# Four interleaved attention layers on one core: GpSimd's long instructions made to wait for VectorE's last short one, the key weights third in the load queue, six extra unread matmuls, and a new written-out order

## The chip, the core and the metric

The kernel runs on one core of a Trainium2 chip. Time is device time of that core in microseconds (us). Five engines work side by side, each through its own list of instructions in the order in which the kernel wrote them: TensorE (PE; its weight loads are listed apart as PEld), VectorE (DVE), ScalarE (ACT), GpSimd (POOL), and SyncE (SP), which here only issues DMAs. They are held together by semaphores. A wait stands at the head of one engine's list, so whatever is queued behind the waiting instruction on that engine waits too.

## The reference

Four layers follow one another on x, 2048 tokens by 512 features: A, B, A, B. Each is normalised first and added to x.

```python
def _A_ref(x, wqkv, wo):            # linear attention, 32 heads of 16
    phi = lambda t: jnp.where(t > 0, t + 1, jnp.exp(t)) + 1e-6
    pq, pk = phi(q), phi(k)
    kv = einsum("bhsd,bhse->bhde", pk, v);  z = einsum("bhsd->bhd", pk)
    o = einsum("bhqd,bhde->bhqe", pq, kv) / (einsum("bhqd,bhd->bhq", pq, z) + 1e-6)
    return o @ wo
def _B_ref(x, wqkv, wo):            # softmax attention in a window of 256 tokens back
    mask = (i - j >= 0) & (i - j < 256)
    p = softmax(where(mask, q @ k.T * 16 ** -0.5, -1e9))
    return (p @ v) @ wo
x = x + A(norm(x)); x = x + B(norm(x)); x = x + A(norm(x)); x = x + B(norm(x))
```

Both A layers use one set of weights, both B layers another.

## The kernel before, in words

The 2048 tokens are cut into 16 tiles of 128, and x stays on the chip throughout. `Plan` writes the whole program down as a graph of some 2500 steps (`Op`), each with an engine or a choice of engines, what it reads and writes, and the PSUM bank tiles that it uses. Four stages can be told apart in time, with their edges running into one another:

- **First A layer.** Per tile `norm` takes statistics (`stats`, `aggr` on VectorE), the inverse root of the variance on GpSimd (`eps`, `pow`), normalises (`xn`, VectorE), and transposes (`T`). `a_k` and `a_q` are matmuls (`k`, `q`), and `phi` makes their feature map by an exponential on ScalarE (`E`) and two VectorE steps (`E1`, `phi`). `g` gathers normalised x times keys.
- **First B layer.** `front` makes the output of the A layer for a tile (`aout`, then `res` adds it to x), its norm, and q, k, v of the B layer (`bq`, `bk`, `bv` on TensorE, then the evictions `bqe`, `bke`, `bve`, each on ScalarE or on VectorE). Keys and values go to a layout of their own by DMAs (`kd`, `vd`, on SP). `b_scores` makes scores (`s`, TensorE) and their exponential (`ex`, ScalarE), and masks the near triangle on VectorE (`mk`). `b_far` does the same for the far 64 columns of the window; its two masks per tile (`mf`) can be on GpSimd (`affine_select`) or on VectorE (a product with a constant triangle). `b_values` multiplies by the values (`pv`), and divides (`rcp`, `div`). `b_out` transposes by DMA (`oT`), multiplies by `wBo` (`bout`) and adds (`res`).
- **Second A layer**, which begins tile by tile behind the first B layer, and **second B layer**, which begins behind that. The last tile ends in `b_last`, and the result leaves by `outp` (GpSimd or SP) and `out` (SP).

What sets the order is not the code but a table. `place` unpacks `TABLE`: two bytes per step give the order of all steps, one byte per step its engine, one byte per tile its PSUM bank. `place` also adds the waits that reuse of a bank needs, and `synchronise` turns all of them into semaphore waits. Each engine then plays its steps in the order of the table. In `setup` the loads are listed as x's first tile, the key weights `wAk`, and so on, but here, too, the order in which SP issues them is the table's. Ten matmuls named `fill` that nobody reads run at the start, from `fill()`, behind nine more that `run` itself writes; a first group of constants is made by GpSimd in `setup`, and the others in `consts` (`c3` to `c24`, and `wp`, which rearranges B's weights).

Of the kernel before, what the change touches and what calls it, by code (L numbers as in the profile page):

```python
# [11 lines left out]
P = 128  # L12
D = 512
# [73 lines left out]

def place(g):
# [116 lines left out]
LATE = 5  # L205
FILL = 10
# [7 lines left out]
class Plan:  # L214
# [33 lines left out]
    def fill(self):  # L248
# [4 lines left out]
        for i in range(FILL):  # L253
            ps = Tile(1, K.cls)
            self.pe("fill", lambda e, ps=ps: e.matmul(K.ps(ps), K.warm[:, 0:P], K.warm, start=True, stop=True), -1000.0, 1, 512, ps=[ps])
            for o in first:
                o.deps.append(self.g.ops[-1])

# [340 lines left out]
    def b_scores(self, j, b, fs, key):  # L599
# [3 lines left out]
        q = P * j + 64 * b  # L603
# [3 lines left out]
        pair = lambda two, free: bass_view(K.PS[:, two[0].banks[0], :], [[512 * (two[1].banks[0] - two[0].banks[0]), 2]] + free)  # L607
# [12 lines left out]
        out = lambda h, m, w: bass_view(K.P(sl)[:, h, fs[0], 384 * b:384 * b + w], [[2816, m], [704, n], [1, w]])  # L620
# [7 lines left out]
        def mk(e):  # L628
            x = out(0, 4, 64)
            return e.tensor_tensor(x, x, K.tri[:, 0, :].unsqueeze(1).unsqueeze(1).to_broadcast([P, 4, n, 64]), ALU.mult)  # L630

        self.on("DVE", "mk", mk, key + 0.02, dve(256 * n, "2x"), rd=[("P", sl, f, b, h) for f in fs for h in range(2)] + [("tri",)], wr=[("P", sl, f, b, 2) for f in fs])

    def b_far(self, j, key):
# [4 lines left out]
        pair = lambda two, free: bass_view(K.PS[:, two[0].banks[0], :], [[512 * (two[1].banks[0] - two[0].banks[0]), 2]] + free)  # L639
# [22 lines left out]
        for b in range(2):  # L662
            def mk(e, eng, b=b):
                x = bass_view(K.P(sl)[:, 0, 0, 384 * b + 256:384 * b + 320], [[704, 16], [1, 64]])
                if eng == "POOL":
                    return e.affine_select(out=x, in_=x, compare_op=ALU.is_ge, fill=0.0, base=-2, pattern=[[0, 16], [-2, 64]], channel_multiplier=1)  # L666
                return e.tensor_tensor(x, x, K.tri[:, 1, :].unsqueeze(1).to_broadcast([P, 16, 64]), ALU.mult)

            engs = {"DVE": dve(1024, "2x")}
            if K.par["gp"]:  # L670
                engs["POOL"] = (1260, 1320)
            else:
                mk = lambda e, mk=mk: mk(e, "DVE")
            self.g.add("mf", engs, mk, key + 0.02 + 0.01 * b, rd=[("F", sl, 0), ("F", sl, 1), ("tri",)], wr=[("F", sl, b, 1)])

    def b_values(self, j, h, key):
# [6 lines left out]
        for f in (2 * h, 2 * h + 1):  # L683
# [66 lines left out]
    def middle(self, ph):  # L750
# [9 lines left out]
        self.rp = 4 if last else 3  # L760
        if last:
# [14 lines left out]
        for j in range(T):  # L776
            if j + 3 < T:
                front(j + 3)
            if j + 1 < T:
                self.b_v(j + 1, (j + 1) % ring, base + j + 1 - par["k_v"])  # L780
            wide = [2, 2]
# [7 lines left out]
            if j + 2 < T:  # L789
                self.b_far(j, base + j + par["k_far"])  # L790
# [26 lines left out]
    r"{cng-pPB;a5@iY{LmoOA>!(E7taWF0tzJi%B3+_NZOpED|QDJ&43`1Zj6oJ?92J&M8EQoI*C%lIS5C+3yIBW=wpaR6h3@E6v5`@S2m;enX#CKpZ0%pWv",
    r"5D^PuB20{#Ff(SstmrT@mW2{f7>i(0EC$7JI26ackPjkZ63h?Ta0Dd9>{t>jVF|2&L7_U<!17oVYhgvq19h-6mV+u-0GeV|tcJ~S1=PlsP!O793v7eKu",
    r"rjp7Rj?ZBVm+*n4e$(9g~r$#&q7IPg5{whHo`T~3U@&e*bRGNFI0r#I08rFIhcu~a5T=s1NZ@E;~cyPV{j~v!?}1L=HYx?h5KMN9>g`c02ktToPcYwEq",
    r";V4cpe@=JKT+X@B&Q5y|@pj;dGpclW;P&$8|UZ*W*JtgpXhYZp2NvA3woTT!tNR5q8AS&;^%cCtQq6@FJFmOL!R%;}HymEAb0l!|Qkj17l|lM1koBuD~",  # L820
    r"F46p!I?Jb^{1C>5ii^awZO7K}_=F$f05VDtnZV-$)?&oDSW$6y$pLQrwIira8Ip2Uz8ieBI?yn{P%C*H){cnVMB87xj`aTlJ$64VvD;d#7^aVQ>@q*8Q",
    r"(PSPp5fTgJ_#icS-jjB@&8b-tEDaNE~@DfK*Xc|ees0JmWFqD+S(kpz8Z}2T9!%>usl4A-yP4Ouu-oyL&08`;Zj7G631*M|TSeD9Bc?w72DJ4aqnpBHw",
    r"(`Xt)V`&^Epfhxq&QU^2M2V>arKaT6jLuUXsz}XgI#r?;G=nZsJ(@`ks4jiMuUMbHVH!$H-!UD%Lm(ugoAd$G(|i1gx9B!SqVY6=m?lyyYC~D6A(g_?*",
    r"qT~WTe?V>=o4P143vo?QZ~v?Ij9jerY58)BQ>R*l$qvG70N<o@CsF?Ni>;qQCTd9^Jp&3r`(i>^3oK_M?#tmSz17juF^GXM^P{;wx?ONh!#?JoK1@<8g",
    r"`)Q*pXJy5{iLKX&J4e<+PG|U>{sV-Ki(8qx@8W)>0@A&AqTU7Nphmh@Q}T3d4n{Foop}w2|)6CVEUy=^eeN&GdnGQhBbx6}b}Mqx<xcD)U`>Ks~4@<-n",
    r"Yn3wu#G4$l#|6Lq1f)SLQHU&@XBs0u%%*c^v%a%akeU1<tO<Vf5XUr~SRhXZIT$K^LPjc@U7-bJrz3vH#{)Qz6e9(qevxf*Yy=k$VJ(si27NjMqrpih*",
    r"PBlBKL!29SkeW9-ug%fd9PR<EAF%P6cG?>!x5E@GRDH^BcX%wAfaCNTD2Pgv{q;#B->+lV#%QHAWZztvyoRU*<YEI8hITJVInLLYUb91i2HMthI<W_u#",
    r"@A5s)%!-9IH(<k-9S7nTe27|eJpM-CDHb>6IoybWk+X1C?#P`v8)xUde3*_<6Yk2yZTLQS;x4?Dm+^9L%kB6m9i#4ioVxKUUd@5IJ$K+99Fre#5YET>x",
    r"d0dB#=MT#@LKN4>$w;A=03cE7jO>F$%S|!&*gbsm=|$>9K=PqC>P^goQJpZ4t~Y2c_Yu~H#`7`;6omW^>`3&=b#*ngYzyPjPX=_wVQKuao)oTR0%H0A-",
    r"FI1<Hh`lA9F~q&ri4%m*#{jk?PNTIk8Hj2Jm1W!iV@U59MLJi8pg&wS_<PRzAYRc?2g_BY7Y<QD3>K+R4pSbM=&4sAv3~NAXJj!r%Bkf8c%GQtjshe2_",  # L830
    r"o#3dL%rQtA`0QliqU6`Vn3RL3}(TCKEN!lT)!@0?tLa>}X{Dy7PzvZ<`<I0sU#)CoSxV|Xl&<5PT^-*R@9L*-O!)JsmKTB~<_hR<?pl}3%{3H*Wss~`$",
    r"h5tUhy%B6y;U@D9{$LG1d>Y#F~x2l-xs0yeHTvQcT?^Gdml;5j7DzEyWKB`Zur^=)Xs=}&`YO6}9b}FALsq(8*s<-;Ada1Rluj;41sCBBeTCc*Y{wkab",
    r"uPUktDx$i`m-sSY;YjK#2Uj6gTGd5$RU1?{wNvd<Bh_v-K!s50)Mz!4`>4n&ii)Z#smiK~8l}ppNnB1%=1yviDyz1rt!kU9s;a4>YPbrmLaBjjkou|yt",
    r"0Ahos-b$Q?y9D$rG}}EYJ}RS4ya9Pv)Zo?s%R>@I;0M(BkCGo=NlYDRZwHqI5l3KQ|HxDrNzhuWhJIUA&I3rd*yygT~HTQZB<8|R%g^%RbCxabyYoeT%",
    r"AxSRbaWK>Z>4fSzS@VWty6<_NuEYsLW8oWTu*>Ldb0OO@){53S^E7DG?--WR{3BQB6{l)gF~aZmYS<Ndq-c1(JrUk-DSqs(b3bdY~Sv$kI%jOKcTILdh",
    r"c)Rko{Z>bi=fZm6khzIq@cJJbRdO%|#}Dz0iF4<)w5kw~&w#g&6{NS3I>GDU@!FcMZCNp8t2kL8Idi7w$JkHnDd@>m^_m=a5}$x%5b`6P#&lG9RHa>`P",
    r"*Or4RUl0b^cS;-~wq_`|sC8dPiROjTp+*0|afE1G_s=aiOr}9j)N<k?k9i_Fjl~U44+DJlqE{P<ul$J8mQj$n3DJ$iqiu9It(pO$cA9*QHReX7-Ua8mW",
    r"xq6|x%Nx~Mx=0x=%P&<|=^_23r_7XDGF!SyIZi6cB)J@y6Vgk{O9iPYmE@$Pkd)G221r#ID1)T3RFmpbLu$%YnJ&}hy?l^bQd{cCQdus8Wtn%xTH*aOS",
    r"tyI-mAsZY@<!522ALs4WT-5bxl&h_$VyoyZ)KQdlzEa$hRbS6Eo)?ijFeF_Ulzzm`6L%)t<;nH@>$k-+u~>$BTBEA4YE<*$wj#&m*t9Fm1|O4Z<5WjMH",
    r")*J5uHZTN>jNmH)O1gldZB%w#y_*Ck>>bOqLz8Pj*Tp*)QW|g4EHwWQy#TiLyub%1yZ?x8;u9m3wkP?n_4fMRMs3`m21C96Fm0tF!CeI*-n)zYFM`I-k",  # L840
    r"y@!|BXAi_WUGHrncfI=?QU>*{*Cy{@kt=vum=ZlpWtj(VUDtUKu-I;akz2kFMTi4Lhd>tNdHrh0~+shjEGx{L0r1L;<}n;xvg>j-*?9;%1w;kvbMquc6",
    r"sx{xlcyXzi$vYw)6>4<uSo~ozmBD%S5p<C)cy07l1i|S%JlrFAI=$^Wl4y{Y-k-E3urKjsKdbS>=FX)SUx89>i>vejA9-!ywxq7|6q{rxSdc2;X$LbI!",
    r"q}itr=y`g+zO1k4l{%COZNixTdV#*Guj%W0m0qn2m}k16DP;ERgF2GFp(E=TdZS*bpX*I}i{7jk>B1(uj-kVvn0m1;Vjk)!I-Ch_9_eHHgkGy3>*G4AU",
    r"ZR)kW%{PRr6=mWI+~89W9!>`jozv!={x$BzN=sBm?oCFr{Cz<rj#zNBbZP6v;LwF>BIVnKB^;{NamaVuAl0cx~M5;w&~*Lt=_J8=!ANwPNcyk*6;Lt9n",
# [179 lines left out]
```

## Time and profile before

| | |
|---|---|
| runs | 420.35, 420.37 and 419.5 us; median 420.35 |
| profiled execution | span 418.7 us from the first to the last instruction; its own time outside the profiler isn't given, and the median lies 1.65 us above the span, the lowest run 0.8 us |
| TensorE busy | 395.0 us, 94% |
| VectorE busy | 352.5 us, 84% |
| ScalarE busy | 345.2 us, 82% |
| GpSimd busy | 137.6 us, 33% |
| granted TensorE clock | 0.995 on the mean |

Busy time is the time in which the engine has an instruction in work. Matmuls overlap one another in the record (a 512-column one is shown with 380 ns, and the next starts 216 ns after it), so a busy TensorE isn't one at its peak. The chain of waits is followed back from the last instruction: each piece is what released the next one. A row of the timeline gives start, duration, engine, line and operation, and in brackets the idle time of the engine before it and what ended that. Lines are those of the kernel before. L382 is all matmuls with tokens as rows (`k`, `v`, `aout`, `bv`, `bout`), L396 those with features as rows (`q`, `bq`, `bk`), L614 and L649 near and far scores, L691 `pv`; L624 and L658 the exponentials; L630 `mk`, L667 `mf` on VectorE, L666 `mf` on GpSimd, L347 `xn`, L406 `E1`.

### The profile page before, as it was taken

What the parts mean: (1) busy time and instruction counts of PE and PEld (TensorE: products, weight loads), DVE (VectorE), ACT (ScalarE), POOL (GpSimd) and SP (SyncE); (2) the same over time, 40 slices, a digit from 0 to 9 for tenths busy, and PEclk for the clock granted to TensorE, in tenths of its full rate; (3) what the DMA queues carried; (4) which work ended last, traced back from release to release, by engine and by line L of the source; (5) the groups of instructions that cost most, each with busy time, mean ns of one, the idle gap of its engine ahead of it and who ended that gap; (6) DMA issues with size and microseconds to landing.
All of it is one profiled execution on the core that took longest, in us unless ns stands there. A gap on an engine that the chain in (4) does not pass through costs nothing.

```text
span 418.7 us, 17187 instructions
## 1 busy us (share of the span) xinstructions
PE 395.0 (94%) x7549; PEld 258.8 (62%) x7549; DVE 352.5 (84%) x788; ACT 345.2 (82%) x428; POOL 137.6 (33%) x227
## 2 busy tenths in 40 slices
PE   8999999999999999999999999999999988989975
PEld 3644775776575567465567677676667646657634
DVE  6997899989989898988886989898898696866655
ACT  3524459999999999889996247999999999999983
POOL 5578522140433252311603302321234241243011
PEclk9999999999999999999999999999999999999989
DMA  7675025432344345343232002343324333244552
GB/s 233 196 176 139 2 71 126 104 92 55 78 92 92 80 99 100 77 100 87 67 68 39 16 2 78 73 98 93 80 54 117 81 80 80 53 122 127 129 95 64
DMA packets 67842, 37.81 MB, mean 90 GB/s; under 512 B 48248, under 2 KB 62968, under 8 KB 67768
## 3 DMA queue, kind: packets, MB, share of 16 engines
q1 hardware_dynamic: 67472, 35.93, 35.5%
q8 instruction: 59, 0.97, 1.0%
q0 software_dynamic: 288, 0.79, 0.6%
q14 instruction: 15, 0.12, 0.1%
q10 hardware_dynamic: 8, 0.00, 0.0%
HBM read 6.29 MB, written 2.10 MB: 20 GB/s over the span
## 4 chain that ended last, share of the span: by engine, by line
PE 54%; ACT 28%; DVE 10%; DMA 4%; issue 2%; POOL 1%; SPq 1%; POOLq 0%; ACTq 0%
PE ps L382 19%; ACT pb L624 18%; PE ps L396 14%; PE ps L691 9%; PE ps L614 5%; ACT pb L658 4%; ACT vp L624 4%; PE ps L457 3%; DVE stats L343 2%; DMA xres<-in_A_x_dram 1%; ACT vp L658 1%; DMA oT<-o 1%; DVE pb L630 1%; DVE tE L406 1%; DVE xres L550 1%
## 5 line engine op out<-in xcount | busy, mean ns | idle before, releaser
L624 ACT ACTIVATE pb<-ps 128x1024 bf16<-128x1024 f32 (+2 forms) x224 | 207.6, 1024 | 9.9 <-PE ps L614 8.7
L691 PEld LDWEIGHTS ps<-vB,pb 128*128 128x128 bf16 x2560 | 77.7, 96 | 12.3 <-issue 4.6
L691 PE MATMUL ps<-vB,pb 128*128 128x34 bf16 x2560 | 82.9, 178 | 1.7 <-DVE vS L371 0.7
L345 POOL TENSOR_SCALAR ve<-mv 128x1 f32<-128x1 f32 x64 | 15.4, 240 | 189.8 <-DVE mv L344 188.3
L396 PE MATMUL ps<-xT,wBp 128*128 128x128 bf16 x1024 | 69.3, 220 | 1.6 <-ACT pb L624 0.6
L396 PEld LDWEIGHTS ps<-xT,wBp 128*128 128x128 bf16 x1024 | 58.4, 97 | 12.6 <-issue 6.9
L666 POOL TENSOR_SCALAR_AFFINE_SELECT pb<-pb 128x1024 bf16<-128x1024 bf16 x43 | 50.1, 1165 | 43.3 <-ACT pb L658 41.4
L405 ACT ACTIVATE tE<-ps 128x512 bf16<-128x512 f32 x64 | 37.8, 606 | 29.7 <-PE ps L382 12.9
L614 PE MATMUL ps<-XQ,kB 32*128 32x256 bf16 (+2 forms) x1024 | 49.8, 268 | 8.4 <-ACT pb L624 3.1
L630 DVE TENSOR_TENSOR pb<-pb,tri 128x512 bf16<-128x512 bf16 x112 | 50.9, 464 | 5.6 <-ACT pb L624 5.3
L382 PE MATMUL ps<-wA,XQ 128*128 128x512 bf16 x192 | 48.8, 380 | 2.0 <-DVE XQ L371 0.9
L658 ACT ACTIVATE pb<-ps 128x1024 bf16<-128x1024 f32 x50 | 49.3, 1059 | 0.4 <-PE ps L649 0.3
L550 DVE TENSOR_TENSOR xres<-ps,xres 128x512 bf16<-128x512 f32 x63 | 43.0, 684 | 7.6 <-PE ps L382 7.0
L343 DVE BATCH_NORM_STATS2 stats<-xres 128x6 f32<-128x512 bf16 x64 | 43.6, 686 | 3.4 <-DMA xres<-in_A_x_dram 2.4
L346 POOL TENSOR_TENSOR rs<-ve,negh 128x1 f32<-128x1 f32 x64 | 37.9, 592 | 5.3
L614 PEld LDWEIGHTS ps<-XQ,kB 32*128 32x128 bf16 x1024 | 15.6, 92 | 37.5 <-ACT pb L624 14.1
L382 PE MATMUL ps<-wBo,oT 128*128 128x512 bf16 x124 | 33.4, 387 | 2.1 <-DMA oT<-o 1.8
L382 PE MATMUL ps<-wBv,xT 128*128 128x512 bf16 x128 | 33.7, 381 | 0.8 <-DVE xres L550 0.4
L396 PE MATMUL ps<-XQ,wA 128*128 128x128 bf16 x512 | 34.4, 220 | 0.0
L396 PEld LDWEIGHTS ps<-XQ,wA 128*128 128x128 bf16 x512 | 30.3, 98 | 5.1 <-issue 0.6
L382 PE MATMUL ps<-M,XQ 128*128 128x512 bf16 x128 | 33.0, 381 | 0.4 <-DVE xres L550 0.2
L382 PEld LDWEIGHTS ps<-wA,XQ 128*128 128x128 bf16 x192 | 16.6, 97 | 20.6 <-DVE XQ L371 1.1
(107 smaller groups left out, 525.6 us busy)
## 6 DMA issues: line engine op xcount, KB each, us to landing
vB<-vS SPq DMA_DIRECT2D x64, 136.0 KB, 2.5
kB<-vp SPq DMA_DIRECT2D x64, 128.0 KB, 2.1
wA<-in_A_wqkv_dram SPq DMA_DIRECT2D x3, 512.0 KB, 6.0
out_dram<-xres SPq DMA_DIRECT2D x9, 128.0 KB, 2.6
xres<-in_A_x_dram SPq DMA_DIRECT2D x2, 512.0 KB, 6.0
pb<-in_B_wqkv_dram SPq DMA_DIRECT2D x1, 1024.0 KB, 6.3
xres<-in_A_x_dram SPq DMA_DIRECT2D x3, 256.0 KB, 3.2
out_dram<-xres POOLq DMA_DIRECT2D x6, 128.0 KB, 2.4
```

The costliest lines, as they stand in the source:

```text
L343: self.on("DVE", "stats", lambda e: e.bn_stats(K.stats[:, t, :], K.xres[:, t, :]), key, dve(512), rd=[("xres", t)], wr=[("stats", t)])
L346: self.pow = self.on("POOL", "pow", lambda e: e.tensor_tensor(K.rs[:, t, :], K.ve[:, t, :], K.negh[:], ALU.pow), key + 0.03, (640, 690), r ...
L382: m = e.matmul(K.ps(ps), lhs(c), rhs(c), start=c == 0, stop=c == 3)
L396: m = e.matmul(K.ps(ps)[:, f * P:(f + 1) * P], w(c, f), xT(c), start=c == 0, stop=c == 3)
L405: self.on("ACT", "E", lambda e: e.activation(K.tE[:, s, :], K.ps(ps), ACT.Exp, bias=0.0), key, act(512), wr=[("tE", s)], ps=[ps])
L550: self.on("DVE", "res", lambda e: e.tensor_tensor(K.xres[:, t, :], K.ps(po), K.xres[:, t, :], ALU.add), key, dve(512), rd=[("xres", t)], w ...
L614: m = e.matmul(K.ps(ps[gq])[:, ns * i:ns * i + ns], K.kB[rows, j % 4, 2 * f + b, :, :], K.XQ[rows, f, q:q + ns], start=True, stop=True, ti ...
L624: return e.activation(out(2 * h, 2, ns), i, ACT.Exp, bias=0.0, scale=0.25)
L630: return e.tensor_tensor(x, x, K.tri[:, 0, :].unsqueeze(1).unsqueeze(1).to_broadcast([P, 4, n, 64]), ALU.mult)
L658: return e.activation(far(h), i, ACT.Exp, bias=0.0, scale=0.25)
L666: return e.affine_select(out=x, in_=x, compare_op=ALU.is_ge, fill=0.0, base=-2, pattern=[[0, 16], [-2, 64]], channel_multiplier=1)
L691: m = e.matmul(K.ps(ps)[:, 34 * u:34 * u + 34], K.P((b // 2) % rp)[:, gq, f, o:o + P], K.vB[:, (b // 2) % 4, b % 2, r, :], start=i == 0, s ...
```

## The change

**Waits.** `place` gets a last loop over the order. Whenever a GpSimd step of the list LONG comes, it is made to wait for the last VectorE step of the list SHORT that stands ahead of it in the order.

**Matmuls.** `fill()` adds six more matmuls of 512 columns that nobody reads, with `wBo` as both operands. Where they run is the table's.

**New code that isn't used.** `PACK`, `QUAD`, `SUMMED` are empty and `MASKS` is 0, so `b_edge` is never called, `packed` is always false and `sh` is 0; `b_scores`, `b_far` (its masks now in `far_masks`) and `b_values` write the same instructions as before.

```diff
+LONG = ("mf", "zero", "wp", "c6", "c9", "c10", "c14", "c21", "c24")
+SHORT = ("xn", "mk", "md", "ma", "mf", "E1", "recb")
...
@@ def place(g):
             held[x.banks[0]] = x
+    before = None
+    for o in order:
+        if o.eng == "DVE" and o.name in SHORT:
+            before = o
+        elif o.eng == "POOL" and o.name in LONG and before and before not in o.deps:
+            o.deps.append(before)
     return order
...
+KEEP = 6
+MASKS = 0
+PACK = {}
+QUAD = ()
+SUMMED = ()
...
@@ def fill(self):
+        for i in range(KEEP):
+            ps = Tile(1, K.cls)
+            self.pe("fill", lambda e, ps=ps: e.matmul(K.ps(ps), K.wBo[:, 0, 0:P], K.wBo[:, 1, :], start=True, stop=True), 1000.0, 1, 512, rd=[("wBo",)], ps=[ps])
...
@@ def b_scores
+        packed = j in self.packed
+        sh = 32 * packed
...
@@ def b_values
+            rd += [("A", i % K.rp) for i in range(max(0, j - 2), j + 1)]
...
@@ TABLE: all of its lines are replaced
```

**The table, unpacked by the rule of `place`.** The steps are numbered as the graph makes them, so that both tables can be set side by side. These are all the steps whose engine differs:

| step | from, to | how many, and the tiles (B layers: 0 to 15 the first, 16 to 31 the second) |
|---|---|---|
| `mf`, far masks | GpSimd to VectorE | 20 (first B layer 10, second 10); on VectorE 27 of 56 instead of 8 |
| | VectorE to GpSimd | 1 |
| `bqe` | VectorE to ScalarE | tiles 2, 12, 18, 20; the other way tile 7 |
| `bve` | VectorE to ScalarE | tiles 2, 4, 10, 11, 19; the other way tile 22 |
| `bke` | ScalarE to VectorE | tiles 3, 12, 18, 19; the other way tile 11 |
| `ve`, `recb` | VectorE to ScalarE | one each |
| `ge`, the last tile's first `oTe` | ScalarE to VectorE | one each |
| `outp` | SP to GpSimd | 6; the other way 3 |

The new loop adds a wait to 54 GpSimd steps: 29 far masks, 8 `wp`, 12 constants, 5 `zero`. The six new matmuls stand at places 127 to 312 among TensorE's 874 steps, all in the first B layer. The heads of two lists, before (first) and after (second), where `x0` is the load of tile 0, `x2` that of tiles 2 and 3, `x4`, `x6`, `x8`, `x12` further ones, and `k0`, `k1` are the two halves of the key matmuls of tile 0, `k2`, `k3` those of tile 1:

```text
SP     x1 x0 x2 x4 wAk x6 wAq x8 T5 x12 wBn T7 T6 T9 T8 wAo wAv ...
SP     x0 x1 wAk x2 x4 wAq x6 x8 x12 T5 wBn T7 T6 T8 T9 T11 T10 wAo ...
TensorE  fill x10, T1 T0 T2 k0 k1 k4 T3 k2 k3 k5 q0 q1 q2 q3 k6 k7 g0 ...
TensorE  fill T0 fill fill k0 T1 k1 fill fill fill fill k2 k3 q2 T2 q0 q1 fill k4 T3 fill k5 ...
```

And the ends of three lists (`bout60`, `bout61` are of tile 14 of the second B layer, `oT31`, `oT32`, `oTe1`, `oTe2` and `bout62` to `bout64` of the last tile; `oT28` is tile 12 of that layer):

```text
TensorE  ... pv126 pv127 oT31 bout60 bout61 oT32 bout62 bout63 bout64
TensorE  ... pv126 pv127 oT31 bout60 oT32 bout61 bout62 bout63 bout64
VectorE  ... rcp62 div62 rcp63 div63 res62 res63 res64
VectorE  ... rcp62 div62 rcp63 oTe1 div63 res62 res63 res64
SP     ... oT27 kd60 vd60 vd61 outp10 oT28 oT29 outp6 vd63 vd62 outp11 oT30 outp14 out0 out1
SP     ... kd63 kd61 oT27 oT28 vd60 vd61 vd63 oT29 vd62 oT30 out0 out1
```

Elsewhere the steps stand in much the same succession as before, each shifted by a few places.

More of the change, by code (lines that the diff above doesn't have):

```diff
@@ new lines, in far_masks, with mk @@
+    def far_masks(self, j, key, also=()):
+        K = self
+        sl = j % self.rp
+        for b in range(2):
+            def mk(e, eng, b=b):
+                x = bass_view(K.P(sl)[:, 0, 0, 384 * b + 256:384 * b + 320], [[704, 16], [1, 64]])
+                if eng == "POOL":
+                    return e.affine_select(out=x, in_=x, compare_op=ALU.is_ge, fill=0.0, base=-2, pattern=[[0, 16], [-2, 64]], channel_multiplier=1)
+                return e.tensor_tensor(x, x, K.tri[:, 1, :].unsqueeze(1).to_broadcast([P, 16, 64]), ALU.mult)
+            self.g.add("mf", {"DVE": dve(1024, "2x"), "POOL": (1260, 1320)}, mk, key + 0.02 + 0.01 * b, rd=[("F", sl, 0), ("F", sl, 1), ("tri",)] + [x for x in also if x[3] == b], wr=[("F", sl, b, 1)])
@@ L660, in b_far @@
             self.on("ACT", "ex", ex, key + 0.01 * h, act(1024), wr=[("F", sl, h)], rd=[("P", sl, 0)], ps=[ps[2 * h], ps[2 * h + 1]])
[L662 to L674, printed above, removed]
+        self.far_masks(j, key)
     def b_values(self, j, h, key):
@@ L788, in middle @@
                     self.b_values(j, h, base + j + (h + 1) / 2 + par["k_pv"])
-            if j + 2 < T:
+            if j in self.packed:
+                self.far_masks(j, 0.0, [("P", j % self.rp, f, b, h) for f in range(4) for b in range(2) for h in range(2)])
+            elif j + 2 < T:
                 self.b_far(j, base + j + par["k_far"])
@@ L817 @@
[L817 to L820, printed above, removed]
```

159 lines of the change are left out of this document (100 added, 59 removed).

## The prediction

> **What bounds the kernel now.** I read the chain of waits first, by engine, then busy time by stage (first A layer, first B layer, second A layer, second B layer, end; length, then busy time and instructions of PE, PEld, DVE, ACT and POOL, granted clock, share of the DMA engines, GB/s), then the chain inside the first B layer.
>
> ```profile
> PE 54%; ACT 28%; DVE 10%; DMA 4%; issue 2%; POOL 1%; SPq 1%; POOLq 0%; ACTq 0%
> ```
> ```profile
> 0.00:57.00 57.00, 54.80 (x515) 31.86 (x516) 49.07 (x118) 22.62 (x40) 35.76 (x75) 1.00 0.50 137
> 57.00:232.00 175.00, 169.32 (x3425) 111.19 (x3423) 156.96 (x353) 161.53 (x193) 53.01 (x84) 1.00 0.37 85
> 232.00:296.00 64.00, 62.84 (x1099) 44.18 (x1098) 58.01 (x122) 48.64 (x65) 17.08 (x28) 1.00 0.24 61
> 296.00:400.00 104.00, 96.10 (x2258) 64.20 (x2254) 78.36 (x175) 102.80 (x115) 30.09 (x38) 1.00 0.39 93
> 400.00:418.70 18.70, 11.92 (x262) 7.36 (x262) 10.07 (x23) 9.65 (x17) 1.63 (x3) 0.88 0.33 80
> ```
> ```profile
> by line: PE ps L382 23.6%; PE ps L691 16.4%; PE ps L396 16.2%; ACT pb L624 11.3%; PE ps L614 8.6%; ACT pb L658 4.3%; DVE pb L630 2.3%; DMA xT<-xn 2.1%; PE ps L649 1.8%; DVE XQ L539 1.4%; issue 1.3%; DVE xn L347 1.2%; DVE xres L550 1.1%; DVE
> ```
>
> The last line is the chain between 57 and 232. TensorE carries 66.6% of it (23.6 + 16.4 + 16.2 + 8.6 + 1.8), ScalarE 15.6%. Both, and VectorE, are busy for about nine tenths of that stage (169, 162 and 157 of 175 us), so no single engine can be sped up for much. From 296 to 400 ScalarE alone is the bound: 102.8 of 104 us.
>
> VectorE is a tenth of the chain, and part of that tenth is not work. These are four of seven such pieces of the whole chain, the first and the last among them (start, us, what), and then the usual durations of the same lines (min/median/max in ns):
>
> ```profile
> 119.52 1.09 DVE pb L630 x2
> ...
> 173.39 2.24 DVE pb L630 x2
> 180.13 1.33 DVE xn L347
> ...
> 294.91 1.16 DVE tE L406
> ```
> ```profile
> L630 DVE TENSOR_TENSOR pb<-pb,tri x112: 360/416/1349, 69.1 to 406.5; 128x512 bf16<-128x512 bf16 x112
> L406 DVE TENSOR_SCALAR tE<-tE x64: 235/284/1226, 11.1 to 302.0; 128x512 bf16<-128x512 bf16 x64
> L347 DVE TENSOR_SCALAR xn<-xres,mv,rs x48: 322/404/1330, 53.7 to 369.3; 128x512 bf16<-128x512 bf16 x48
> ```
>
> Two L630 back to back take some 0.75 us (0.36 + 0.42, first minimum, then median: the second shows its end as well). Over that, the chain loses 0.3 at 119.5, 1.5 at 173.4, 0.9 at 180.1, 0.6 at 204.0 (an L406), 0.5 at 238.1 and 0.9 at 292.1 (L347), and 0.9 at 294.9: **5.6 us**. VectorE at one of these places, and GpSimd at two:
>
> ```profile
> 173.31 2.47 DVE L630 TENSOR_TENSOR pb<-pb,tri 128x512 bf16<-128x512 bf16 x2
> ```
> ```profile
> 173.09 2.42 POOL L666 TENSOR_SCALAR_AFFINE_SELECT pb<-pb 128x1024 bf16<-128x1024 bf16 x2 [0.84 <-ACT pb L658]
> ...
> 180.17 1.15 POOL L666 TENSOR_SCALAR_AFFINE_SELECT pb<-pb 128x1024 bf16<-128x1024 bf16 x1
> ```
>
> The stretched `xn` ends at 181.46, 0.14 after the mask at 181.32; the two stretched `mk` end at 175.78, 0.27 after the masks at 175.51. So a short VectorE instruction that meets a far mask on GpSimd ends only behind it. [...]
>
> **The change part by part.**
>
> *Long behind short, and the new order.* I unpacked both tables and summed, behind each far mask on GpSimd, the VectorE work listed up to the next short step (0.6 for a step over 512 elements, 0.35 for `div`, 0.2 for `rcp`, from start to start in the timeline). Before, 32 of 48 masks have under 1.0 us there, and the shortfalls to one mask (1.15 us) add up to 24.7 us; after, 16 of 29, and 7.5 us. That is 70% less, so of the 5.6 us I take 70%: **-3.9**. Bounds: 0 if the freed time is only waited elsewhere, -5.6 if no meeting is left. Late next at these places is the matmul that VectorE fed, or ScalarE. The new wait itself I cost at nothing: GpSimd is busy 137.6 of 418.7 us. Queued behind the waiting mask stand `eps` and `pow` of a later tile (within three steps for 26 of 29 masks), and `xn` waits for those; today it does so for 2.0 us in all:
>
> ```profile
> DVE xn L347 <- POOL rs L346: 2.0, 2, 1.7
> ```
>
> Without that cover each of the 26 would add up to one L630, 0.42 us: at most +11.
>
> *Masks to VectorE.* 19 more on the net, at the median of
>
> ```profile
> L667 DVE TENSOR_TENSOR pb<-pb,tri x7: 676/684/1561, 94.0 to 403.4; 128x1024 bf16<-128x1024 bf16 x7
> ```
>
> 13.0 us of new VectorE work. The evictions that move the other way relieve it by 2.5 (`bqe` -3, `bve` -4, `bke` +3, 0.68 each by the CAST row below, and single ones that add up to +0.2), which leaves +10.5. What hides it is VectorE's idle time, 18 us in the first B layer and 26 of 104 in the second. Uncovered share: VectorE's tenth of the chain, **+1.1**; bounds 0 and +10.5.
>
> *Evictions.* By these rows
>
> ```profile
> L371 DVE CAST XQ<-ps 128x512 bf16<-128x512 f32 x24 | 16.4, 684 | 4.8 <-PE ps L396 4.8
> L567 ACT ACTIVATE vp<-ps 128x512 bf16<-128x512 f32 x10 | 7.6, 761 | 1.1 <-PE ps L396 1.1
> L371 ACT ACTIVATE XQ<-ps 128x512 bf16<-128x512 f32 x8 | 4.8, 598 | 0.8 <-PE ps L396 0.5
> L371 ACT ACTIVATE vS<-ps 128x512 bf16<-128x512 f32 x6 | 4.1, 676 | 1.7 <-PE ps L382 1.7
> ```
>
> ScalarE gains in the first B layer one `bqe` (0.60), four `bve` (2.70), loses one `bke` (-0.76), and takes a `ve` and a `recb` (0.9): +3.4 us, of which its 15.6% of that chain, **+0.5**. In the second B layer it loses two `bke`, gains two `bqe`: -0.3 at almost full share, **-0.3**. Bounds -0.7 and +3.4.
>
> *Six unread matmuls.* The ten of the start take 0.216 us each (2.16 from the first to the next), so 1.3 us; at TensorE's two thirds of the chain **+0.9**, bounds 0 (each falls into idle time) and +1.3.
>
> *Load order and start.*
>
> ```profile
> 0.80 1.94 SPq L269 DMA_DIRECT2D xres<-in_A_x_dram  x4
> 2.78 0.48 SPq L272 DMA_DIRECT2D wA<-in_A_wqkv_dram  x1
> ...
> 4.89 2.32 PE L255 MATMUL ps<-kB 128*128 128x512 bf16 x10
> ...
> 8.85 1.47 PE L382 MATMUL ps<-wA,XQ 128*128 128x512 bf16 x6 [0.64 <-DMA wA<-in_A_wqkv_dram]
> ```
>
> The key weights are issued at 2.78, and `k0` waits for them until 8.85. Third in the queue they are issued two places earlier, at 1.8 (half a us each), so at least 1.0 us is won; and they have 0.52 MB of x less ahead, which at 1.31 MB from the first issue at 0.80 to 8.85 (163 GB/s) is at most 3.2. I take 2.2, `k0` at about 6.6. But the time doesn't fall by 2.2: before, TensorE went on without a gap through six halves `k` (twelve matmuls of 0.216) and a `T`, to 11.7. After, it runs `k0` to `k3`, two `T` and five `fill`, and then meets `q2`, which needs `wAq`; that has 0.26 MB less ahead of it (x6), 1.6 us at the same rate, and was there by 11.7 before, so some 10 us. By 11.7 it is ahead by 0.4 at the best. **-0.3**; bounds -1.0 and +0.8, of which the upper is the last rival below.
>
> *End.* The chain there, and the first `oTe`'s row:
>
> ```profile
> 396.45 5.05 DMA oT<-o
> 401.64 1.02 PE ps L382 x4
> ...
> 405.81 0.85 PE ps L382 x2
> 406.89 0.84 PE ps L382 x2
> ```
> ```profile
> L371 ACT ACTIVATE oT<-ps 128x256 bf16<-128x256 bf16 x2 | 0.8, 384 | 2.7 <-PE ps L726 2.7
> ```
>
> `oT28` was issued at 396.45 behind two 136 KB `vd` and an `outp`, and landed 5.05 us later. After, it stands ahead of both `vd`. TensorE then needn't idle, and the halved clock behind that idle time (two matmuls in 0.85 us instead of 0.43, four such, 0.84 us in all; granted clock 0.88 in the row of this stage) may go with it. That is up to -1.8: 0.84 of clock, and 1.0 of the wait, an estimate, since ScalarE still has work for most of the 5.05. I take half, -0.9. [...] Against it, `oTe1` on VectorE stands ahead of `div63` there, which delays the last transposes by its 0.4. **-0.5**; bounds -1.8 and +0.4.
>
> The sum: -3.9 + 1.1 + 0.5 - 0.3 + 0.9 - 0.3 - 0.5 = -2.5, a span of 416.2. The median of the runs lies 1.65 above the span, so **417.9 us** against 420.35, 0.6% faster. About 0.2% (0.85 us) is what a measurement of this kernel can tell from no change.
>
> **The rivals.**
>
> *VectorE becomes the bound* (slower). The masks' 13.0 us are certain, the freed stalls are not: they are freed only if VectorE and GpSimd keep the table's timing. Were the meetings per mask on GpSimd unchanged, 29 of 48 masks would keep 60% of the 5.6 us, saving 2.2, and if the 6.8 us that ten masks add in the first B layer reach the chain, the sum is -2.2 + 6.8 + 0.8 (the rest without masks and meetings: 0.5 - 0.3 + 0.9 - 0.3, and no gain at the end) = +5.4: **425.7**. For it: VectorE has 157 of 175 us there, and evictions wait in its queue. Against it: the count in the tables. It decides where VectorE is over 95% busy from 57 to 232.
>
> *Freed time is waited for elsewhere* (no change): the 3.9 shrinks to 1.4 since TensorE and ScalarE, nine tenths busy, are late next, and the rest sums to +1.4: **420.4**. That is also how it looks if the waits do nothing.
>
> *The meetings cost more than their pieces on the chain* (faster by more). The group's mean lies above its median of 416 ns:
>
> ```profile
> L630 DVE TENSOR_TENSOR pb<-pb,tri 128x512 bf16<-128x512 bf16 x112 | 50.9, 464 | 5.6 <-ACT pb L624 5.3
> ```
>
> That is 5.4 us of stall (112 times 48 ns) in one line, while the chain shows 1.8 of it. If the stalls off the chain count as well, since each delays a bank's release, the gain may double to 7.8; with the end's full 1.8 and the rest (+1.9) the sum is -7.7: **412.6**.
>
> *TensorE goes cold at the start* (less gain). The ten matmuls that filled 4.89 to 7.05 are spread out, and TensorE may idle ahead of `k0` as it did ahead of 401.64. At the same 0.84 and without the start's gain that is +1.1 on the forecast: **419.0**. [...]
>
> **How the numbers follow.** Forecast 0.37; meetings worth more 0.10; cold start 0.04; no change 0.13; VectorE the bound 0.29; the waits ahead of `eps` and `pow` at half their price (+5.5 on the forecast, 423.4) 0.07. Faster 0.51, same 0.13, slower 0.36. The range of 411.5 to 425.8 reaches from the case of the costlier meetings to VectorE's; the forecast's own is 415 to 419.5.
>
> **What would show it.** Right: no `mk`, `xn` or `E1` over 0.7 us but a handful; L666 29 times, L667 27; VectorE's busy time within 4 us of 352.5; first `k` matmuls near 6.6 and the next wait at `q`; no 5 us transpose at the end. Wrong: stretched rows as many as before; `xn` waiting for GpSimd over 4 us; VectorE over 360 us busy; matmuls of 0.42 us apart after 5 us.

## The result and the profile after

The changed kernel takes a median of **416.65 us** over 14 runs (415.97 to 419.3), the kernel before 419.29 us over 14 runs beside it (417.54 to 420.86): a ratio of **0.994**, interval 0.9921 to 0.9959, so 0.6% faster. The profiled execution has a span of 414.2 us; its own time was 415.97, 0.7 below the median. The two profiled spans differ by 4.5 us, the medians by 2.6. In the profiled execution of the kernel before, the granted TensorE clock is 0.5 for 3.41 us from 404.06 us on and again from 417.71 us to the end, which lowers the mean to 0.995. Of the 69 executions of that kernel timed beside the experiments, 34 have a mean of 0.996 or less (median 419.94 us) and 35 of 0.998 or more (418.35). Of the changed kernel's 14, one has 0.996, and the median of the others is 416.58. Between executions of 0.998 or more the gain is thus 1.8 us.

Busy time by stage of the changed kernel comes first (columns as in the prediction: length, then PE, PEld, DVE, ACT and POOL, granted clock, DMA share, GB/s), then the chain of waits by engine.

```profile
0.00:57.00 57.00, 53.60 (x509) 31.21 (x518) 48.75 (x119) 22.56 (x39) 36.41 (x77) 1.00 0.49 137
57.00:232.00 175.00, 167.81 (x3413) 112.55 (x3447) 153.85 (x361) 164.69 (x202) 41.62 (x73) 1.00 0.39 85
232.00:296.00 64.00, 62.22 (x1103) 44.54 (x1111) 55.24 (x122) 49.26 (x67) 12.71 (x23) 1.00 0.24 63
296.00:400.00 104.00, 94.64 (x2220) 63.19 (x2233) 80.40 (x182) 102.72 (x115) 25.04 (x35) 1.00 0.43 95
400.00:414.20 14.20, 9.66 (x249) 7.01 (x250) 8.53 (x22) 6.55 (x13) 1.95 (x4) 0.98 0.29 80
```
```profile
PE 48%; ACT 35%; DVE 9%; DMA 5%; issue 2%; SPq 1%
```

VectorE does ten far masks more in the first B layer and yet is busy there for 153.9 us instead of 157.0: its short instructions hardly stretch any more, and four evictions fewer fall to it. The second B layer is what it was: ScalarE, 102.7 of 104 us. TensorE's share of the chain fell from 54% to 48%, ScalarE's rose from 28% to 35%. Laid step beside step (by the exponentials on ScalarE), the two profiled executions show where the time went: the changed kernel is 0.4 to 1.1 us behind from 80 to 160 us, level near 170, in the first B layer, mostly 1.3 to 2.5 ahead from 190 to 400 us, and 4.9 ahead at the last exponential.

The short instructions, by line and shape (count, then busy us and mean ns, then idle time before): `mk`, `xn` and the far masks on VectorE and on GpSimd of the changed kernel, and `xn` of the kernel before, whose `mk` row stands in the prediction.

```profile
L652 DVE TENSOR_TENSOR pb<-pb,tri 128x512 bf16<-128x512 bf16 x112 | 44.7, 412 | 4.0 <-ACT pb L644 3.7
L365 DVE TENSOR_SCALAR xn<-xres,mv,rs 128x512 bf16<-128x512 bf16 x48 | 19.4, 405 | 4.1 <-POOL rs L364 3.2 <-DMA XQ<-xn 0.6
L704 DVE TENSOR_TENSOR pb<-pb,tri 128x1024 bf16<-128x1024 bf16 x24 | 16.2, 682 | 0.3 <-ACT pb L732 0.3
L703 POOL TENSOR_SCALAR_AFFINE_SELECT pb<-pb 128x1024 bf16<-128x1024 bf16 x26 | 29.8, 1148 | 62.9 <-DVE pb L652 32.6 <-ACT pb L732 17.7 <-DVE o L766 6.3
```
```profile
L347 DVE TENSOR_SCALAR xn<-xres,mv,rs 128x512 bf16<-128x512 bf16 x48 | 22.0, 459 | 2.1 <-POOL rs L346 2.0
```

The mean of `mk` fell from 464 to 412 ns and that of `xn` from 459 to 405. Counting as stretched each `xn`, `mk`, `mf`, `E1` and `recb` on VectorE that runs over 0.25 us longer than the median of its kind, the kernel before has 19 of them with 12.3 us too much, the changed one 2 with 0.6 us. GpSimd pays with 32.6 us in which its masks wait for an `mk`, which costs nothing by itself as long as the masks still come in time. The rest of this document shows how much hangs on that.

### The profile page after: what moved, and what is told of

Its sections match the earlier page's. It is cut to its first block, busy times and chain, and to the rows that moved or that the text cites. A ratio compares the mean times of both kernels' runs of the same rounds, so it can differ in the third digit from the quotient of the medians.

```text
span 414.2 us, 17130 instructions
## 1 busy us (share of the span) xinstructions
PE 387.9 (94%) x7481; PEld 258.5 (62%) x7555; DVE 346.8 (84%) x803; ACT 345.8 (83%) x432; POOL 117.7 (28%) x211
## 4 chain that ended last, share of the span: by engine, by line
PE 48%; ACT 35%; DVE 9%; DMA 5%; issue 2%; SPq 1%
ACT pb L644 22%; PE ps L400 17%; PE ps L414 13%; PE ps L753 7%; ACT pb L732 6%; ACT vp L644 5%; PE ps L634 5%; PE ps L475 2%; DMA XQ<-xn 2%; DVE stats L361 2%; DMA xres<-in_A_x_dram 2%; DVE xres L568 1%; DVE XQ L557 1%; PE ps L723 1%; ACT vp L732 1%
## 5 line engine op out<-in xcount | busy, mean ns | idle before, releaser
L363 POOL TENSOR_SCALAR ve<-mv 128x1 f32<-128x1 f32 x64 | 16.7, 261 | 172.6 <-DVE mv L362 170.5
L400 PE MATMUL ps<-wA,XQ 128*128 128x512 bf16 x176 | 46.2, 379 | 2.7 <-issue 0.6
L652 DVE TENSOR_TENSOR pb<-pb,tri 128x512 bf16<-128x512 bf16 x112 | 44.7, 412 | 4.0 <-ACT pb L644 3.7
L703 POOL TENSOR_SCALAR_AFFINE_SELECT pb<-pb 128x1024 bf16<-128x1024 bf16 x26 | 29.8, 1148 | 62.9 <-DVE pb L652 32.6
L400 PE MATMUL ps<-wBv,xT 128*128 128x512 bf16 x112 | 31.5, 380 | 2.2 <-issue 1.3
L400 PE MATMUL ps<-wBo,oT 128*128 128x512 bf16 x105 | 28.8, 380 | 4.2 <-issue 1.1
L400 PE MATMUL ps<-M,XQ 128*128 128x512 bf16 x112 | 30.7, 380 | 2.1 <-issue 1.0
L765 DVE RECIPROCAL rc<-ps 128x16 f32<-128x16 f32 x64 | 16.1, 252 | 19.3 <-PE ps L753 19.0
```

The lines of the kernel that those rows point to most:

```text
L400: m = e.matmul(K.ps(ps), lhs(c), rhs(c), start=c == 0, stop=c == 3)
L652: return e.tensor_tensor(x, x, K.tri[:, 0, sh:64].unsqueeze(1).unsqueeze(1).to_broadcast([P, 4, n, 64 - sh]), ALU.mult)
```

## The experiments

Eleven kernels ran. Each was timed beside runs of the kernel before, whose medians were 419.24 us (beside the waits without the new table, the new table without the waits, the new table with the old loads, and the transpose at the end), 418.96 (the masks on VectorE in the old table, back on GpSimd in the new one, and no unread matmuls) and 419.54 (the other four). Where a "slip" is given, the same steps of two profiled executions are set against each other.

### The waits without the new table, and the new table without the waits

The kernel before with the two lists and the loop, its order, engines and banks as they were:

```
 def place(g):
...
+    before = None
+    for o in order:
+        if o.eng == "DVE" and o.name in SHORT:
+            before = o
+        elif o.eng == "POOL" and o.name in LONG and before and before not in o.deps:
+            o.deps.append(before)
     return order
```

> The kernel before, with its own table, and only the new loop of waits. If the waits themselves end the meetings, the stretched VectorE instructions (over 0.7 us, some 19) fall to a few, and the kernel gains 1 to 3 us. If it is the table that keeps long and short apart, the waits change little: a meeting in which the short step comes after the long one is not touched by them, stretched rows stay at 12 or more, and the time stays within 0.8 us of 419.3 or rises by up to 2, since masks and what is queued behind them start later.

Measured: **443.09 us**, ratio 1.0568 (1.0534 to 1.0603), 24 us slower, which neither expectation had. The waits did what they say, since the stretched instructions fell from 19 with 12.3 us to 8 with 4.6. But they put something dearer in their place. Waits of this kernel, by engine and line, waited-for engine and line (us in all, times, longest):

```profile
POOL pb L676 <- DVE pb L640: 81.6, 16, 13.9
...
PEld ps L701 <- POOL pb L676: 22.9, 12, 3.6
PE ps L701 <- POOL pb L676: 19.3, 12, 3.4
```

GpSimd's masks wait 81.6 us for `mk`, and TensorE's value products `pv` (L701) then wait for the masks, which they hardly did before (their weight loads, 0.5 us in all). Matmuls and weight loads wait for the same thing at the same time, so the two rows are one loss of about 20 us. The other part is the clock. Stages of this kernel around two such places, with the granted clock in the third column from the end:

```profile
190.00:197.00 7.00, 3.99 (x64) 2.35 (x61) 4.78 (x12) 5.39 (x7) 1.29 (x1) 1.00 0.29 61
197.30:200.80 3.50, 3.50 (x109) 2.85 (x105) 1.47 (x4) 1.65 (x2) 0.00 (x0) 0.51 0.02 5
200.80:224.70 23.90, 20.25 (x388) 11.89 (x386) 17.49 (x39) 20.46 (x24) 6.59 (x8) 1.00 0.28 70
224.70:228.10 3.40, 3.07 (x28) 1.69 (x27) 0.82 (x3) 2.91 (x4) 0.00 (x0) 0.50 0.00 0
```

TensorE idles in front of a late mask, and the next 3.4 us run at half speed. The slip is 6 us at 190 us and 14 at 230.

The other way round, the changed kernel with those lines of `place` taken out:

```
-    before = None
-    for o in order:
...
-            o.deps.append(before)
     return order
```

> The changed kernel, its new table, without the loop of waits. If the waits matter, stretched rows come back (8 or more) and it loses 1 to 3 us against 416.65. If the table alone does it, there are under 6 stretched rows and the time is within 0.8 us of 416.65.

Measured: **425.86 us**, ratio 1.0154 (1.0123 to 1.0184). The new table without its waits is 6.6 us slower than the old kernel, and the waits win 9.2 us in it. The stretched instructions are back: 20 with 13.0 us. `xn` by line and shape, then a piece of the chain of waits (start, us, what), and GpSimd at that place in the timeline:

```profile
L359 DVE TENSOR_SCALAR xn<-xres,mv,rs 128x512 bf16<-128x512 bf16 x48 | 27.4, 573 | 3.3 <-POOL rs L358 2.4 <-DMA XQ<-xn 0.7
```
```profile
324.86 1.69 DVE pb L646 x2
326.55 0.92 DVE xn L359
```
```profile
325.08 2.48 POOL L697 TENSOR_SCALAR_AFFINE_SELECT pb<-pb 128x1024 bf16<-128x1024 bf16 x2
```

Two masks of GpSimd, from 325.08 to 327.56, stretch two `mk` to 1.69 us and the `xn` behind them to 1.23. At the same steps the changed kernel has 0.75 and 0.41, with GpSimd's mask behind the `xn`:

```profile
317.79 0.75 DVE L652 TENSOR_TENSOR pb<-pb,tri 128x512 bf16<-128x512 bf16 x2
318.46 0.41 DVE L365 TENSOR_SCALAR xn<-xres,mv,rs 128x512 bf16<-128x512 bf16 x1
```
```profile
318.94 1.15 POOL L703 TENSOR_SCALAR_AFFINE_SELECT pb<-pb 128x1024 bf16<-128x1024 bf16 x1 [1.00 <-DVE xn L365]
```

The slip of the run without waits grows by 1.5 us at just this place (7.07 to 8.59), and by similar steps at the other stretched groups: 1.5 around 40 us, 0.9 at 114, 2.7 between 150 and 160, 0.7 at 241. In all 9.2 us of median are lost for 12.4 us of stretch, 0.75 us for each; the expectation had 1 to 3. The profiled execution, which holds no whole window at half clock, loses 8.7 (424.64 against 415.97); the other four, at a granted clock of 0.995 or 0.996, seem to hold one each.

### Which waits, and why they hurt the old order

The changed kernel with the waits in front of the masks alone:

```
-LONG = ("mf", "zero", "wp", "c6", "c9", "c10", "c14", "c21", "c24")
+LONG = ("mf",)
```

> The changed kernel with the wait only in front of the far masks; zeroing, constants and weight copies wait for nothing new. Theory A, each stretched piece of VectorE costs about 0.7 of its length where it stands: the first layer's four stretched pieces come back (2.2 us, which cost 1.8 in the run without any waits), so 418 to 419 us, and VectorE's rows after 60 us stay at two or three long ones. Theory B, the whole gain of 9 us is from the first layer's waits and what follows from an early start: above 422 us.

Measured: 419.03 us, ratio 0.9989 (0.9963 to 1.0015). So the masks' waits carry 6.8 of the 9.2 us, and those of the zeroing, the constants and the weight copies 2.4. The four stretched instructions of the first layer are there again (2.2 us), with a slip of 1.6 us between 31 and 45 us, and so are an `xn` of 0.83 and one of 0.42 us too much between 238 and 268 us, where 0.6 is lost.

The kernel before with the waits, but none in front of the twelve masks for which TensorE stood:

```
+FREE = (1, 6, 14, 16, 18, 20, 23, 31, 37, 38, 50, 53)
...
-        elif o.eng == "POOL" and o.name in LONG and before and before not in o.deps:
+        elif o.eng == "POOL" and o.name in LONG and before and before not in o.deps and o not in free:
             o.deps.append(before)
```

> The kernel before with the new waits, but without the wait for the twelve far masks (numbers 1, 6, 14, 16, 18, 20, 23, 31, 37, 38, 50 and 53) whose end TensorE stood waiting for in the run with all waits (idle 0.45 to 3.43 us each, 19.5 us together). Theory A, the loss of 24 us is that a waiting mask reaches its value product too late, and TensorE's half clock after such a gap: most of it comes back, 418 to 424 us, the granted clock at 0.99 or more, TensorE waiting less than 5 us for a mask of GpSimd. Theory B, the loss is in the waits themselves wherever they stand (constants, zeroing, GpSimd's chain of means behind them): at least 435 us, the clock below 0.98.

Measured: **429.75 us**, ratio 1.0253 (1.0211 to 1.0295), clock 0.991. More than half of the loss comes back (13.3 of 23.9 us), yet it is outside what either theory gave. What is left is told by GpSimd's timeline at one place of this kernel, and TensorE's:

```profile
311.63 3.58 POOL L680 TENSOR_SCALAR_AFFINE_SELECT pb<-pb 128x1024 bf16<-128x1024 bf16 x3 [13.84 <-DVE pb L644]
```
```profile
314.04 0.24 PE L705 MATMUL ps<-vB,vp 128*128 128x34 bf16 x2 [3.43 <-POOL pb L680]
```

GpSimd stood for 13.84 us in front of the first of three masks, whose `mk` came late. The third is one of the twelve and waits for nothing, but it is third in GpSimd's queue; in the kernel before the same three ran from 292.08 to 295.91. Four of the twelve are late in this way, with the same idle times of TensorE as in the run with all waits (2.33, 2.29, 3.43 and 0.93 us, 9.0 together). With 1.8 us lost in the first layer that covers the remaining 10.2. So the loss is late masks, as theory A has it, and its number failed by leaving out what is queued behind a wait.

### The masks on VectorE, one part at a time

The twenty masks that the new table puts on VectorE instead of GpSimd, moved in the old table, and moved back in the new one (`far` counts the masks as they are listed):

```
+MOVED = (0, 1, 4, 8, 11, 20, 22, 23, 25, 27, 29, 31, 34, 35, 45, 46, 48, 49, 50, 53)
...
         o.eng = ("PE", "ACT", "DVE", "POOL", "SP")[raw[2 * n + o.i]]
+        if o.name == "mf":
+            far += 1
+            if far - 1 in MOVED:
+                o.eng = "DVE"
```

(with `"POOL"` in the last line for the new table).

> The kernel before, its own table, with the same 20 far masks on VectorE and no new waits. If fewer masks on GpSimd alone bring the gain, stretched rows fall from 19 to 11 or fewer and it gains 1 to 3 us on 419.3. If VectorE's 13 us more reach the chain as the rival had it, it loses 2 to 6 us.

> The changed kernel with the 20 far masks that had moved to VectorE back on GpSimd, at the same places in the order, with their waits. If the moved masks are part of what ends the meetings, 8 or more stretched rows come back, and it loses 1 to 3 us against 416.65. If VectorE's 13 us more of masks only cost, it gains up to 1 us.

Measured: on the old order **443.54 us**, ratio 1.0562 (1.0518 to 1.0606); moved back on the new one 419.7, ratio 1.0007 (0.9981 to 1.0034). Neither expectation had the loss of 24 us on the old order. There a moved mask stands in VectorE's queue where it suited GpSimd, and is late there too, with the same end, a halved clock. Waits of this kernel (the old order, masks moved) and two of its stages:

```profile
PEld ps L698 <- DVE pb L674: 10.2, 5, 3.4
PE ps L698 <- DVE pb L674: 8.5, 5, 2.9
```
```profile
210.30:217.10 6.80, 5.81 (x116) 3.88 (x118) 3.21 (x9) 3.88 (x4) 0.07 (x1) 0.50 0.19 40
```

In the new order the twenty moved masks are a gain of 3 us, not a cost: back on GpSimd, where each waits for a short instruction, one of them is late again, and TensorE idles 1.15 us for it and then has one window at half clock. That makes 1.5 of the 3.3 us of slip; the rest comes in small steps, 0.6 around 95 us, 0.4 at 134 and 0.9 around 230. The half clock isn't what the 3 us rest on, for in 7 of the 12 executions the granted clock is 0.998 or more, without such a window, and their median is 419.44. Nor do the meetings come back: 2 stretched instructions with 0.9 us are in this run, where 8 or more were expected. TensorE's timeline, and the window behind it:

```profile
116.51 1.35 PE L760 MATMUL ps<-vB,pb 128*128 128x34 bf16 x48 [1.15 <-POOL pb L710]
```
```profile
118.20:121.70 3.50, 3.50 (x72) 3.05 (x73) 1.88 (x5) 3.39 (x4) 2.83 (x3) 0.51 0.22 78
```

Both parts together in the old order, that is the first edit and `MOVED` in one kernel:

> The kernel before with both the new waits and the 20 far masks on VectorE, in the old order. Theory A, only an order made for both lets the masks come in time: of the twelve late masks six stay on GpSimd and six go to VectorE behind its old queue, so TensorE still waits over 10 us for masks and the time is 430 to 450 us. Theory B, the two parts complete each other (fewer GpSimd masks to wait, fewer meetings): 422 us or less.

Measured: **451.51 us**, ratio 1.0773 (1.0725 to 1.0821), slightly slower than theory A's range. The stretch is nearly gone (6 instructions, 2.8 us), and TensorE waits for masks of both kinds:

```profile
PEld ps L708 <- POOL pb L683: 12.3, 7, 3.4
PEld ps L708 <- DVE pb L684: 10.1, 5, 2.9
```

So no part completes another without the order that was made for it.

### Load order, unread matmuls, the end

The changed kernel with the nine loads in the old order, and the kernel before with the first six in the new one:

```
+    loads = ("x1", "x0", "x2", "x4", "wAk", "x6", "wAq", "x8", "x12")
+    at = [k for k, o in enumerate(order) if o.name in loads]
+    for k, name in zip(at, loads):
+        order[k] = next(o for o in ops if o.name == name)
```
```
+    loads = ("x0", "x1", "wAk", "x2", "x4", "wAq")
+    order = [next(o for o in ops if o.name == name) for name in loads] + [o for o in order if o.name not in loads]
```

> The changed kernel with x's and the weights' loads in the order of before. If the early key weights are worth what the prediction said (0.3 us), it is within 0.8 us of 416.65, and the first exponential of the first B layer starts within 0.8 us. If the late x tiles behind the key weights are what made the first layer end 0.4 to 0.9 us later than before, it gains about that. If the first key matmuls at 6.6 instead of 8.9 do count, it loses 1 to 2 us.

> The kernel before with the first six loads in the changed kernel's order (x0, x1, key weights, x2, x4, query weights), all else as before. As predicted for this part: 0.3 us faster, 418.7 to 419.2 against 419.1. By the comparison of the changed kernel with and without the old load order (medians 416.65 and 418.98): 2.3 us faster, about 417. By a third way, the old table cannot use the key weights early, since its first transposes and projections stand in the old order: no faster, and with x2 and x4 landing later up to 1 us slower.

Measured: 418.98 us, ratio 0.9994 (0.9972 to 1.0017), for the new table with the old loads; 420.42 us, ratio 1.0032 (1.0006 to 1.0058), for the old table with the new loads. The new load order is worth 2.3 us in the new table and costs 0.9 in the old one. TensorE's start in the timeline, of the changed kernel, of the same with the old loads, and of the kernel before with the new loads:

```profile
6.56 0.60 PE L400 MATMUL ps<-wA,XQ 128*128 128x512 bf16 x2 [0.26 <-ACT XQ L384]
...
9.44 0.62 PE L414 MATMUL ps<-XQ,wA 128*128 128x128 bf16 x8
```
```profile
8.23 0.59 PE L404 MATMUL ps<-wA,XQ 128*128 128x512 bf16 x2 [1.20 <-DMA wA<-in_A_wqkv_dram]
...
11.04 0.61 PE L418 MATMUL ps<-XQ,wA 128*128 128x128 bf16 x8
```
```profile
8.70 0.40 PE L361 MATMUL ps<-ident,vp 128*128 128x128 bf16 x4 [0.58 <-DVE vp L349]
9.68 0.40 PE L361 MATMUL ps<-ident,vp 128*128 128x128 bf16 x4 [0.58 <-DVE vp L349]
9.91 1.46 PE L384 MATMUL ps<-wA,XQ 128*128 128x512 bf16 x6
```

The first `k` moves from 8.23 to 6.56, but by 24 us the gain is down to about 0.7 and stays there to the end of the profiled execution (0.6). In the old table the transposes of three tiles stand ahead of the first `k`; two of them wait for tiles that are now normalised later, `k` begins at 9.91 instead of 8.85, and 0.7 to 1.0 us are lost up to 390 us; in the profiled execution the last layer's end makes up for it, in the medians it doesn't. The other 1.7 us between the medians of the changed kernel with its own and with the old loads are in no step of these profiles, but in the clock: with the old loads the granted clock is 0.996 in 8 of 12 executions (median 419.17), as much as one window at half clock takes away (half of 3.41 us, 1.7 us), and 0.998 or more in the other four (417.10), the profiled one among them. With its own loads the changed kernel has such a window in one of 14, and 416.58 in the median of the others. So without that window the load order is worth 0.5 us, which is the slip; where the window lies, and why the old loads bring it, no trace shows.

The changed kernel without the six unread matmuls:

```
-KEEP = 6
+KEEP = 0
...
-    n = len(ops)
-    order = [ops[raw[2 * k] + 256 * raw[2 * k + 1]] for k in range(n)]
+    n = len(ops) + 6
+    order = [raw[2 * k] + 256 * raw[2 * k + 1] for k in range(n)]
+    order = [ops[i] for i in order if i < len(ops)]
```

> The changed kernel without the six unread matmuls in the first B layer (the ten of the start stay). By the prediction they cost two thirds of 1.3 us, so it gains 0.9 us on 416.65. If they fall into idle time of TensorE, the time is within 0.4 us. If they keep something from going idle, such as the clock, it loses, and a lower granted clock shows in the first B layer.

Measured: 417.22 us, ratio 0.9962 (0.9938 to 0.9986), against 0.994 (0.9921 to 0.9959) with them. By the two ratios they are a gain of 0.9 us, with an uncertainty of 1.3 (the intervals' half widths taken together), so no cost is seen and no clear gain. The granted clock stayed at 0.998 to 1.0 without them, and the 1.5 us by which the profiled execution without them falls behind at one place (80 to 88 us) are a late transfer: its chain there reads

```profile
78.23 4.07 DMA kB<-vp
```

where the changed kernel's chain has only matmuls. One execution can't say whether the matmuls have to do with that.

The kernel before with `oT28` ahead of the two `vd` and the `outp` in SP's queue:

```
+    behind = [[o for o in ops if o.name == "vd"][60], [o for o in ops if o.name == "vd"][61], [o for o in ops if o.name == "outp"][10]]
+    order = [o for o in order if o not in behind]
+    k = order.index([o for o in ops if o.name == "oT"][28]) + 1
+    order[k:k] = behind
```

> The kernel before with one move in SyncE's queue near the end: the transpose oT28 ahead of vd60, vd61 and outp10. If the late transpose and the halved clock behind it cost the end its time, the transpose lands in some 2.5 us instead of 5.05, no pair of matmuls of 0.85 us is left there, and the kernel gains 1.0 to 2.5 us on 419.3. If ScalarE's own work sets the end, or the DMA engines are late anyway, it gains under 0.4 us.

Measured: 419.33 us, ratio 0.9995 (0.9974 to 1.0016), no gain. The 5.05 us transpose is gone from the chain, and ScalarE stands in its place. Chain of waits of this kernel (start, us, what):

```profile
382.16 14.24 ACT pb L628 x16
396.40 1.83 ACT pb L662 x2
398.23 1.83 ACT pb L628 x2
400.06 1.83 ACT pb L662 x2
401.90 0.71 ACT pb L628
```

ScalarE runs without a gap to 402.6, where the transpose let TensorE go on at 401.64. The half clock is there as before: the mean granted clock is 0.995, and two matmuls of 512 columns on the chain take 0.97 us at 405.48, where a pair takes 0.43 at full clock. About half of what the new table has won by the end was won ahead of it: its ScalarE has done the same exponentials by 400.45, 2.2 us earlier, since the layer began earlier. Behind that its lead over this kernel grows to 3.8 us at the last exponential, and no window of the changed kernel is at half clock while it computes (granted 1.00 up to 413.5 us; its last matmul is done at 410.6, its last VectorE step at 411.5). What keeps that window away no run shows by itself.

## Why the prediction came out right, step by step

The forecast was 417.9 us and 2.5 us gained; 416.65 and 2.6 gained were measured. The mechanism that it rests on was seen: long and short instructions hardly meet any more (19 stretched instructions before, 2 after). Most of what was to show it came true. L703 runs 29 times and L704 27 (26 and 3, 24 and 3 by tile); `k0` starts at 6.56, and the next wait for a load is `q2`'s weights at 9.44, for 0.39 us; no 5 us transpose holds up the end. Two signs failed without harm. VectorE is busy 346.8 us, 5.7 less than before where 4 was the limit: the durations of its masks add 12.1 us, those of `xn`, `mk` and `E1` fall by 10.7 and the rest by 2.0, and 5 us more of its instructions overlap in the record and are counted once. And `xn` waits for GpSimd 3.2 us in the row that had 2.0 and 1.3 more in that of the tiles whose result stands in a buffer named `vp`, together over the 4 that were to mean wrong; without the new waits it is 3.7, so the waits add 0.8. But several terms of the sum were wrong and made up for one another:

- *Long behind short, and the new order*, -3.9. The waits are worth **-9.2** in the new table. The term that was mis-sized is this price: only the pieces on the chain of the kernel before were counted, 5.6 us, and 70% of them. The new table without its waits has 13.0 us of stretch, and each of them costs 0.75 us of time. The count of VectorE work behind each mask in the table promised 70% less, but the new table without the waits has as much stretch as the old kernel (13.0 us against 12.3): only the waits hold long behind short.
- The wait itself, costed at nothing with "GpSimd is busy 137.6 of 418.7 us" as cover. In this order that is nearly right: `xn` waits 0.8 us more by it, and TensorE 0.3 us for a mask of GpSimd. As a reason it is wrong: in the old order GpSimd is as idle, and the same waits cost 24 us. What covers a wait is the slack of the mask in front of its value product, and the prediction named `eps`, `pow` and `xn` as those who wait, not `pv`. It took the new order to be right without having shown it.
- *Masks to VectorE*, +1.1. Measured **-3.0** in the new table, a gain. That masks off GpSimd needn't wait is the likely reason, shown for one of them (the 1.15 us). The rival that VectorE becomes the bound falls with it: VectorE is busy for 88% of the first B layer (153.9 of 175 us), where over 95% was to decide for it.
- The other side of these two: what is left, all terms but the waits, was summed to +1.4, and the new table without waits is **+6.6**. More stretch isn't the reason, as said; which part of the table is, evictions or order, or whether the same stretch costs more in this order, no run tells apart.
- *Six unread matmuls*, +0.9: measured -0.9, give or take 1.3. Two thirds of TensorE's chain was too dear a share, as far as that can be told. Five of them have a record in the trace; behind two TensorE waits on (the next matmul starts 455 and 312 ns later instead of 216), so these cost nothing, as the lower bound had it.
- *Load order and start*, -0.3. `k0` and `q2` came as worked out, and the profiled executions have 0.6 to 0.7; the medians have 2.3, and the difference is a window at half clock that most executions with the old loads hold, by their mean clock (0.996 in 8 of 12).
- *End*, -0.5: the transposes' turn in the queue is worth nothing by itself (419.33 against 419.24). The clause "ScalarE still has work for most of the 5.05" was the whole truth: it has work for all of it. The term was too small even so: in the profiled executions the lead grows by 2.7 us between 385 us and the last exponential (2.1 to 4.9), of which a half-clocked window can make up 1.7 (half of its 3.41 us, an estimate); half of the executions of the kernel before (35 of 69) don't hold it, and no run tells what removes it.

The time came out right by luck: the waits' gain and the new table's own loss were both missed by some 5 us, with opposite signs. Of the rivals, "the meetings cost more than their pieces on the chain" was right in its mechanism and not in its time, and the cold start didn't come: the granted clock was 1.00 from 3.96 to 413.5 us.

## What to carry to other kernels

A wait that keeps two engines apart costs what the waiting instruction's consumer lacks in slack, and what is queued behind it lacks, however idle its engine is (in the old order matmuls waited 19.3 us for masks, with GpSimd busy 136 of 443 us): ask of each who reads its result next, and when. In a schedule written out as a whole, parts don't have prices of their own: here the same waits are worth -9 us in one order and +24 in the other, so a part is tried in its own order, by leaving it out. And where the busy engine is TensorE, a gap of a microsecond or two may be paid again in the window behind it, at half clock: here, behind gaps of 1.15 us (masks back on GpSimd) and 2.29 us (waits in the old order), the granted clock was 0.51 for 3.5 us and 0.50 for 3.4.

## What the runs showed of the hardware

The half clock comes in windows of 3.41 us on a fixed grid: in the kernel before from 404.06 to 407.47 us and again from 417.71 us, with 10.24 us (three windows) between; in the changed kernel from 413.56 us only, behind 409.60 us (120 windows) at full clock. Each run has a beginning of its own for it, 4.70 us behind the first instruction in the kernel before and 3.96 in the changed one. Taking TensorE's busy share (the time with at least one matmul in the record) in each full-clock window of the thirteen profiled executions that has a whole window behind it: of 20 windows below 0.5 the next one was at half clock in 18, of 41 from 0.5 to 0.7 in 8, of 1,490 from 0.7 up in none. The changed kernel's emptiest window ahead of the last 4 us has 0.74, the one at 400.6 us in the kernel before 0.44, with the half clock behind it.

In the record the stretched `xn` at 180.13 starts 0.04 us ahead of the GpSimd mask that it ends behind; the pair of `mk` at 173.31 starts 0.22 behind its mask. So at these two places the stretch is told by the ends, 0.14 and 0.27 us behind the masks', and not by the starts; why an instruction is held so, no run shows.

Not expected: one late transfer (the `kB<-vp` of 4.07 us above) puts a whole execution back by 1.5 us, and none of it is made good in the 330 us behind it.
